# One kernel's output gradient: loaded in four parts, multiplied by the gate row once in SBUF, and w2's gradient copied out by ScalarE

## The chip, the cores and the metric

The kernel runs on one core of one Trainium2 chip. The time is device time of one execution in microseconds (us). The kernel before was run six times: 428.01, 429.35, 428.42, 432.36, 431.66 and 432.61, median 430.51. Less is better.

The engines are named as the profile names them: PE (TensorE, matrix products), DVE (VectorE), ACT (ScalarE), POOL (GpSimd) and SP (SyncE). SP computes nothing; here it issues most of the DMA transfers. Each engine works through its own instructions in a fixed order, and an instruction that waits holds up all that is behind it on that engine.

## The reference

The forward pass is a transformer-like block over x of 2048 rows of 512, conditioned by a vector c: six rows of 512 (sa, ca, ga, sb, cb, gb) come out of c and w_mod. The kernel computes the block's output and the gradients of nine inputs (x, the two halves of the spectral weight, w1, b1, w2, b2, c and w_mod).

```python
    h = _layernorm(x, axis=-1) * (1 + ca) + sa
    x = x + ga * _A_ref(h, A_w_r, A_w_i)      # irfft2(rfft2(h) * W)
    h = _layernorm(x, axis=-1) * (1 + cb) + sb
    x = x + gb * _B_ref(h, B_w1, B_b1, B_w2, B_b2)   # relu(h w1 + b1)^2 w2 + b2
```

With g the gradient of the output, two gradients matter here. That of w2 is the transposed hidden activation (1792 x 2048) times (g * gb), which is 1792 x 512. That of b2 is the sum of (g * gb) over the rows. The row gb is the same for all 2048 rows, so it can be applied to g before the product or to the result after it.

## The kernel before, in words

Everything is bf16 in SBUF and fp32 in PSUM. The 2048 rows lie 16 to a partition: t = 0 to 15 names a slice of 128 rows. The transforms are matrix products with tables of sines. The hidden width 1792 is cut in 14 chunks of 128 (fc), the spectrum in 8 groups (gi).

The kernel goes through a forward spectral stage, then the dense stage in four blocks of 512 rows, forward and backward, and from about 280 us on through the backward spectral part. All that the change touches lies in this last part, which has three stages:

- **Spectral stage** (spec_f23, with ew_b at L1164 and after_b at L1172). For each of eight groups PE makes G, DVE multiplies it with the loaded Z and Xb, writing Z in place and gW into a tile with three buffers, and SP stores gW in four pieces (L1170). after_b then loads what comes later and gives PE units of w1's gradient to fill in (grad_w1, L1122, 16 matmuls of 448 columns each). It also runs GMod.emit four times (gms), which makes a piece of w_mod's gradient from tiles wmc and gwm in the pool gmp.
- **G stage** (spec_g1, L336). For each group PE makes two PSUM tiles psG (four buffers); DVE casts one into the big tile CS (L351), ACT the other (L353). Four small casts of psF by DVE and ACT (L365, L367) finish CS.
- **Row stage** (row_pair, L1267, eight times for t = 0, 2, ... 14: eight pairs). PE makes psT and psY from CS; ACT copies them (Tsb at L377, gs at L1276); DVE unfolds gs into gh (L266 to L270), makes gn (L1278) and q (L1281, which reads the loaded rows n), ACT scales gn (L1280), DVE makes two sums (jk, L1285), gn again (L1289), gs (L1290) and the result gx (L1292, which reads the loaded rows gxl). SP stores gx (L1293) and loads n and gxl for two pairs later (load_rows3, L1219). PE sums gh and q over the rows into acc (L1262), two pairs behind. Between pairs, fill gives PE units of w2's gradient.

A unit of w2's gradient is grad_w2 (L1200): 16 matmuls of one fc, with the transposed load hn (L1067, a DMA that transposes) against g_sb, the output gradient g for all 16 slices, 16 KB in each partition. DVE then reads the PSUM result, multiplies it with the row gb (modb at GB_B) and writes gw (L1206), which SP stores (L1207). b2's gradient is made from g_sb by grad_b2 (L1210) and add_quadrants (L1093), with the row gb applied at its end (L1107).

Memory decides when loads can start. Pools are stacks; a tile placed where an older tile was waits for that tile's last reader or writer. g_sb is placed where gmp was.

The order on each engine is not written out by hand. The framework takes the instructions in program order with priorities and lays them out on the engines by its own estimates of durations; tc.issue_after(x) keeps an instruction from being laid out ahead of x. DMA completion on SP is counted by eight semaphores in rotation, so that an issue also waits until the transfer eight places earlier on its queue has landed.

Of the kernel before, what the change touches and what calls it, by code (L numbers as in the profile page):

```python
# [18 lines left out]
D = 512  # L19
# [315 lines left out]

def spec_g1(tc, K, Z, CS):  # L336
    nc = tc.nc
    with tc.tile_pool(name="psG", bufs=4, space=PSUM) as psG_pool, tc.tile_pool(name="psF", bufs=1, space=PSUM) as psF_pool:
        psF = psF_pool.tile([P, 4, P], FP32, name="psF")
        for gi in range(8):  # L340
            for hh in range(2):
                n = 2 * gi + hh
                ps = psG_pool.tile([P, 2, 2 * P], FP32, name="psG")
                for ch in range(2):
                    for ri in range(2):
                        nc.tensor.matmul(ps[:, ch, :], lhsT=Z[gi][:, hh, ri, ch:256:2],  # L346
                                         rhs=K["LG"][:, n, ri:ri + 2, :].rearrange("p y m -> p (y m)"), start=(ri == 0), stop=(ri == 1))
                dst = CS[:, :, :, n, :].rearrange("p t c b -> p c t b")
                src = ps.rearrange("p h (y t b) -> p (h y) t b", y=2, b=8)
                if hh == 0:  # L350
                    nc.vector.tensor_copy(out=dst, in_=src)  # L351
                else:
                    nc.scalar.copy(out=dst, in_=src)  # L353

            if gi % 2 == 1:
                for ri in range(2):
                    for n in range(2 * gi - 2, 2 * gi + 2):
                        q = 32 * (n % 4)
                        nc.tensor.matmul(psF[q:q + 1, n // 4, :], lhsT=Z[n // 2][:, n % 2, ri, 256:257], rhs=K["LG"][:, n, ri + 1, :],
                                         start=(ri == 0), stop=(ri == 1), tile_position=(0, q))  # L360
        for i in range(4):
            dst = CS[0:1, :, 1, i:16:4, :].rearrange("p t m b -> p m t b")
# [81 lines left out]
class GMod:  # L444
# [12 lines left out]

    def emit(self, jc, q, row, pool, ppool):

# [7 lines left out]
        for dc in range(0, 4, 2):  # L467
            wmc = self.tiles[jc][dc // 2]
            gwm = pool.tile([P, 2, D], BF16, name="gwm", bufs=2)
            for i in range(2):  # L470
# [10 lines left out]
def kernel(  # L481
# [586 lines left out]

    lf2 = tc.alloc_tile_pool(name="lf2", bufs=1, side="right")
    gmp = tc.alloc_tile_pool(name="gmp", bufs=1, side="right")  # L1070
    K["LF"] += [lf2.tile([P, 2, 3, P], BF16, name=f"LFb{gi}") for gi in range(4, 8)]
# [20 lines left out]

    def add_quadrants(ps, pool, out, scale=None):  # L1093
        w = ps.shape[-1]
# [5 lines left out]
        def add():  # L1100
# [4 lines left out]
            nc.scalar.copy(out=row, in_=ps[0:1, 0:w])  # L1105
            if scale is not None:
                nc.vector.tensor_tensor(row, row, scale, op=ALU.mult)  # L1107
            nc.sync.dma_start(out, row)
# [5 lines left out]
    def run_later(n=1):  # L1114
        if later:
            later[0][0] -= n
            if later[0][0] <= 0:
                later.pop(0)[1]()

    w1o = {}  # L1120
# [28 lines left out]
    with tc.tile_pool(name="f23b", bufs=2) as fr, tc.tile_pool(name="ewb", bufs=2) as ew:  # L1149
# [22 lines left out]
        def after_b(gi):  # L1172
            if gi + 4 < 8:
                load(gi + 4)
            if gi == 3:
                with tc.issue_after(K["gW"]):
                    nc.sync.dma_start(K["LG"], LG_dram)
            fill_w1(2 if 0 < gi < 6 else 1)
            if gi == 4:
                with tc.issue_after(K["gW"]):  # L1180
                    load_hn()
                    load_hn()
            if gi == 5:
                gmp.release()
                endp["g"] = tc.alloc_tile_pool(name="gsp", bufs=1, side="right")
                endp["g_sb"] = endp["g"].tile([P, NT, D], BF16, name="g_sb")
                with tc.issue_after(K["gW"]):
                    K["g_load"] = nc.sync.dma_start(endp["g_sb"], g_view).ins
            if gi in (0, 1, 3, 4):
                gms.pop(0)[1]()  # L1190
                if len(gms) > 1:
                    gm.load(gms[1][0], gmp)

        spec_f23(tc, K, UT, AEs, None, lambda gi: gwa.tile([P, 2, 2, FP], BF16, name="G", bufs=2), ew_b, after_b)
    g_sb = endp["g_sb"]
    fin = tc.alloc_tile_pool(name="fin", bufs=2, side="right")
    gwp = tc.alloc_tile_pool(name="gwp", bufs=1, side="right")
    endp["gw"] = gwp

    def grad_w2(fc):  # L1200
# [4 lines left out]
        with tc.high_priority():  # L1205
            nc.vector.tensor_tensor(gw, ps, modb[:, GB_B, :], op=ALU.mult)  # L1206
        nc.sync.dma_start(out6_view[:, fc, :], gw)  # L1207
        load_hn()

    def grad_b2():  # L1210
        ps = psX.tile([P, D], FP32, name="mm")
        for t in range(NT):
            q = 32 * (t % 4)
            nc.tensor.matmul(ps[q:q + 32, :], lhsT=K["ones_q"], rhs=g_sb[:, t, :], start=(t < 4), stop=(t >= 12), tile_position=(0, q))
        add_quadrants(ps, gwp, out_7[None, :], modb[0:1, GB_B, :])

    rows3 = {}

    def load_rows3(t):  # L1219
        if t < NT:  # L1220
            rows3[t] = (fin.tile([P, 2, D], BF16, name="n1"), fin.tile([P, 2, D], BF16, name="gxl"))
            nc.sync.dma_start(rows3[t][0], n1_dram[:, t:t + 2, :])
            nc.sync.dma_start(rows3[t][1], gx1_dram[:, t:t + 2, :])

    with tc.issue_after(K["g_load"]):
        load_rows3(0)
        load_rows3(2)
    for _ in range(2):
        load_hn()

    CS = utcs.tile([P, NT, 4, 16, 8], BF16, name="utcs")
    spec_g1(tc, K, Z, CS)
    sp.release()
# [21 lines left out]
    with tc.tile_pool(name="psE", bufs=2, space=PSUM) as psE, tc.tile_pool(name="psS1", bufs=1, space=PSUM) as psS1:  # L1255
# [41 lines left out]
        for t in range(0, NT, 2):  # L1297
# [4 lines left out]
            if t == 10:  # L1302
                grad_b2()
        fill(1)
        late.flush()
# [5 lines left out]
        for j in range(2):  # L1311
            gm.load(j, endp["gm"])
            gm.emit(j, 32 * j, acc1_sb[32 * j:32 * j + 1, :], endp["gm"], psX)
            fill(1)
# [13 lines left out]
    fp.release()  # L1328
    gwp.release()
    fin.release()  # L1330
    endp["g"].release()
    lf2.release()
# [39 lines left out]
```

## Time and profile before

The profiled execution took 428.01 us; its span, from the first to the last instruction, is 426.2 us. It is the fastest of the six runs.

| | whole span |
|---|---|
| PE busy | 397.4 us, 93% |
| DVE busy | 354.6 us, 83% |
| ACT busy | 256.6 us, 60% |
| POOL busy | 54.9 us, 13% |
| mean DMA rate | 237 GB/s |

The places in the last part: the last unit of w1's gradient ends near 357, the first unit of w2's gradient begins at 357.5, the last matmul of the last unit ends at 421.05.

How to read it: a busy share is an average over stages with different limits. For a stage one looks at each engine's busy time in a stretch of it, and at what its waits were for. In the order of time a row has its start, its length, engine, line, operation, out<-in, and in brackets the idle time before it with what ended it. A DMA appears where it is issued, on SP or POOL; when its data land is another number.

### The profile page before, as it was taken

To read this page: it belongs to the slowest core of one execution; us is meant where nothing else is said; L and a number is where in the kernel's file an instruction comes from. 1 tells how busy PE (TensorE), PEld (TensorE's weight loads), DVE (VectorE), ACT (ScalarE), POOL (GpSimd) and SP (SyncE) were. 2 spreads that over 40 slices of the span, in tenths; PEclk is the share of its full clock that TensorE was granted. 3 is DMA by queue.
4 is the path that set the end of the run, shared out by engine and by line. 5 is a ranking of instruction groups with operands and counts; after the bars stand their busy time and mean duration, and the time that the engine had idled before them with its cause. 6 is when DMAs were issued, how large, how long until landed. Compare 5 with 4: busy or idle time off the path is not lost.

```text
span 426.2 us, 7138 instructions
## 1 busy us (share of the span) xinstructions
PE 397.4 (93%) x2375; PEld 195.9 (46%) x2375; DVE 354.6 (83%) x862; ACT 256.6 (60%) x487; POOL 54.9 (13%) x135
## 2 busy tenths in 40 slices
PE   2789989999899999999999999999999999998895
PEld 0345446654434443444444444445655665443332
DVE  6799858968995588978897998956998848999994
ACT  5578699768883179238824776454755465636331
POOL 8347940000000000000000000002121000000011
PEclk9999999999999999999999999999999999999999
DMA  8998899969397459867985998997999989999993
GB/s 237 242 262 270 246 206 316 319 224 238 105 354 249 136 117 291 244 152 158 313 218 172 133 288 295 295 236 240 302 258 329 213 231 220 206 270 267 257 265 115
DMA packets 144227, 101.11 MB, mean 237 GB/s; under 512 B 98969, under 2 KB 127518, under 8 KB 143806
## 3 DMA queue, kind: packets, MB, share of 16 engines
q1 hardware_dynamic: 141034, 93.03, 83.6%
q0 software_dynamic: 2592, 7.09, 5.3%
q10 hardware_dynamic: 564, 0.53, 0.5%
q8 instruction: 19, 0.31, 0.3%
q14 instruction: 18, 0.15, 0.1%
HBM read 35.44 MB, written 41.60 MB: 181 GB/s over the span
## 4 chain that ended last, share of the span: by engine, by line
PE 50%; DVE 21%; ACT 15%; DMA 8%; issue 4%; POOL 1%; ACTq 0%; DVEq 0%; SPq 0%
PE og L906 12%; PE mm L877 10%; PE mm L1126 7%; PE mm L712 5%; PE mm L1203 4%; DMA out_dram<-gW 3%; DMA xs_dram<-Xs 2%; ACT gab L717 2%; PE psG L346 2%; ACT AE L329 1%; DVE jk L1285 1%; ACT Xs L313 1%; PE acc L774 1%; PE psC L311 1%; DVE l_st L817 1%
## 5 line engine op out<-in xcount | busy, mean ns | idle before, releaser
L712 PE MATMUL mm<-gT,w2T 128*128 128x512 bf16 x224 | 57.9, 383 | 2.9 <-ACT gab L717 2.9
L877 PE MATMUL mm<-h2T,w 128*128 128x512 bf16 x224 | 53.4, 378 | 1.4 <-ACT r L879 1.2
L906 PE MATMUL og<-w1T,gab 128*128 128x512 bf16 x224 | 50.9, 379 | 0.8 <-DVE o L971 0.8
L1203 PE MATMUL mm<-g_sb,hn 128*128 128x512 bf16 x224 | 50.4, 379 | 0.4 <-DVE gw L1206 0.4
L1126 PE MATMUL mm<-gab,h_sb 128*128 128x448 bf16 x256 | 50.7, 352 | 0.0
L906 PE MATMUL og<-w,h 128*128 128x512 bf16 x224 | 50.1, 379 | 0.0
L879 ACT ACTIVATE r<-mm,b1col 128x512 bf16<-128x512 f32 x56 | 37.1, 686 | 6.1 <-PE mm L877 3.3
L877 PEld LDWEIGHTS <-w 128*128 128x128 bf16 x224 | 21.1, 97 | 30.0 <-issue 8.3
L1126 PEld LDWEIGHTS <-h_sb 128*128 128x128 bf16 x256 | 24.6, 98 | 21.8 <-issue 0.6
L906 PEld LDWEIGHTS <-h 128*128 128x128 bf16 x224 | 21.8, 98 | 26.1 <-issue 1.0
L1203 PEld LDWEIGHTS <-hn 128*128 128x128 bf16 x224 | 21.2, 98 | 27.2 <-issue 3.6
L906 PEld LDWEIGHTS <-gab 128*128 128x128 bf16 x224 | 21.6, 98 | 25.9 <-issue 1.4
L712 PEld LDWEIGHTS <-w2T 128*128 128x128 bf16 x224 | 21.3, 99 | 22.5 <-issue 6.3
L919 ACT CAST G<-og 128x512 bf16<-128x512 f32 x16 | 9.2, 581 | 28.1 <-PE og L906 28.1
L295 POOL MEMSET AE<- 128x2 bf16 x4 | 0.3, 102 | 194.3 <-PE mm L877 194.3
L1280 ACT ACTIVATE gs<-gn,inv 128x512 bf16<-128x512 bf16 x16 | 11.4, 716 | 21.8 <-DVE gn L1278 21.8
L477 POOL DMA_DIRECT2D out_dram<-gwm x12 | 8.8, 732 | 114.4 <-DVE gx L1292 54.6
L881 DVE TENSOR_TENSOR h<-r 128x1024 bf16<-128x1024 bf16 x28 | 19.2, 687 | 4.8 <-ACT r L879 4.8
L717 ACT CAST gab<-mm 128x512 bf16<-128x512 f32 x36 | 21.4, 602 | 1.9 <-PE mm L712 1.8
L475 DVE SCALAR_TENSOR_TENSOR gm_junk<-wmc,onef,gmbc 128x512 bf16<-128x512 bf16 x24 | 18.0, 748 | 3.2 <-DMA wmc<-in_w_mod_dram 1.6
L715 DVE CAST gab<-mm 128x512 bf16<-128x512 f32 x20 | 13.8, 688 | 7.7 <-PE mm L712 7.4
L1130 ACT CAST gw<-mm 128x448 bf16<-128x448 f32 x16 | 8.6, 540 | 18.4 <-PE mm L1126 18.4
(290 smaller groups left out, 812.2 us busy)
## 6 DMA issues: line engine op xcount, KB each, us to landing
h_dram<-h SPq DMA_DIRECT2D x28, 256.0 KB, 3.2
gh_dram<-gab SPq DMA_DIRECT2D x28, 256.0 KB, 4.3
w<-in_B_w_dram SPq DMA_DIRECT2D x2, 1792.0 KB
wmc<-in_w_mod_dram SPq DMA_DIRECT2D x12, 256.0 KB, 5.5
out_dram<-gwm POOLq DMA_DIRECT2D x12, 256.0 KB, 6.2
wz_dram<-Z SPq DMA_DIRECT2D x8, 258.0 KB, 4.2
xs_dram<-Xs SPq DMA_DIRECT2D x8, 258.0 KB, 4.3
Z<-wz_dram SPq DMA_DIRECT2D x8, 258.0 KB, 5.3
```

Of the source, the lines that this page charges most:

```text
L475: nc.vector.scalar_tensor_tensor(out=junk, in0=wmc[:, i, :], scalar=K["onef"], in1=gmbc, op0=ALU.mult, op1=ALU.mult, accum_out=self.gsc[:, ...
L712: nc.tensor.matmul(ps, lhsT=w2T[:, dc, fc * P:(fc + 1) * P], rhs=gT[b][:, :, dc, :], start=(dc == 0), stop=(dc == 3))
L715: nc.vector.tensor_copy(out=gaT[b][:, fc, :], in_=ps)
L717: nc.scalar.copy(out=gaT[b][:, fc, :], in_=ps)
L877: nc.tensor.matmul(ps, lhsT=w1[:, dc, (fc + i) * P:(fc + i + 1) * P], rhs=h2T[b][:, :, dc, :], start=(dc == 0), stop=(dc == 3))
L879: nc.scalar.activation(r[:, i, :], ps, AF.Relu, bias=b1col[:, fc + i:fc + i + 1])
L881: nc.vector.tensor_tensor(h2, r, r, op=ALU.mult)
L906: nc.tensor.matmul(ps, lhsT=lhs(fc), rhs=rhs[:, fc, :], start=(fc == 0), stop=(fc == NFC - 1))
L919: nc.scalar.copy(out=st["G"][:, j % 2, :], in_=P_.pop(j))
L1126: nc.tensor.matmul(ps[:, 0:W4], lhsT=h2_sb[:, t, dc * P:(dc + 1) * P], rhs=ghn[t // 4][:, t % 4, fs], start=(t == 0), stop=(t == NT - 1))
L1203: nc.tensor.matmul(ps, lhsT=hns[fc][:, t, :], rhs=g_sb[:, t, :], start=(t == 0), stop=(t == NT - 1))
L1280: nc.scalar.activation(gs[:, i, :], gn[:, i, :], AF.Copy, scale=inv1[:, t + i:t + i + 1], accum_out=rr[:, i, 0:1])
```

## The change

1. g_sb is loaded in four DMAs of 512 KB instead of one of 2 MB, in after_b of group 4 instead of group 5 (so gmp is released at group 4, and the GMod piece of that group is emitted before), and ahead of the first two hn loads, which stood there before.
2. In the G stage DVE multiplies each quarter of g_sb in place with the row gb, one after the cast of each of groups 4 to 7 (scale_g, through the new argument after of spec_g1).
3. Since g_sb then holds g * gb, grad_w2 copies PSUM to gw with ACT, without a product, and add_quadrants loses its product.
4. The rows of the first two pairs (n and gxl, four DMAs of 256 KB) are loaded in after_b of group 3 instead of after the spectral stage. Their pool fin is therefore opened before gmp.
5. The wmc tiles for the last two GMod pieces are loaded at t = 10 and not right before each piece; their gwm tile has four buffers instead of two.

```diff
--- before.py
+++ after.py
@@ -333,7 +333,7 @@
         f3(7)
 
 
-def spec_g1(tc, K, Z, CS):
+def spec_g1(tc, K, Z, CS, after=None):
     nc = tc.nc
     with tc.tile_pool(name="psG", bufs=4, space=PSUM) as psG_pool, tc.tile_pool(name="psF", bufs=1, space=PSUM) as psF_pool:
         psF = psF_pool.tile([P, 4, P], FP32, name="psF")
@@ -348,7 +348,7 @@
                 dst = CS[:, :, :, n, :].rearrange("p t c b -> p c t b")
                 src = ps.rearrange("p h (y t b) -> p (h y) t b", y=2, b=8)
                 if hh == 0:
-                    nc.vector.tensor_copy(out=dst, in_=src)
+                    K["cast"] = nc.vector.tensor_copy(out=dst, in_=src).ins
                 else:
                     nc.scalar.copy(out=dst, in_=src)
 
@@ -358,6 +358,8 @@
                         q = 32 * (n % 4)
                         nc.tensor.matmul(psF[q:q + 1, n // 4, :], lhsT=Z[n // 2][:, n % 2, ri, 256:257], rhs=K["LG"][:, n, ri + 1, :],
                                          start=(ri == 0), stop=(ri == 1), tile_position=(0, q))
+            if after:
+                after(gi)
         for i in range(4):
             dst = CS[0:1, :, 1, i:16:4, :].rearrange("p t m b -> p m t b")
             src = psF[32 * i:32 * i + 1, :, :].rearrange("p m (t b) -> p m t b", b=8)
@@ -455,7 +457,7 @@
         for dc in range(0, 4, 2):
             self.tc.nc.sync.dma_start(self.tiles[jc][dc // 2], self.wm_view[:, dc:dc + 2, cs])
 
-    def emit(self, jc, q, row, pool, ppool):
+    def emit(self, jc, q, row, pool, ppool, nbuf=2):
 
         nc, K = self.tc.nc, self.K
         cs = slice(jc * D, (jc + 1) * D)
@@ -466,7 +468,7 @@
         junk = pool.tile([P, D], BF16, name="gm_junk", bufs=1)
         for dc in range(0, 4, 2):
             wmc = self.tiles[jc][dc // 2]
-            gwm = pool.tile([P, 2, D], BF16, name="gwm", bufs=2)
+            gwm = pool.tile([P, 2, D], BF16, name="gwm", bufs=nbuf)
             for i in range(2):
                 if i == 0:
                     nc.scalar.activation(gwm[:, i, :], gmbc, AF.Copy, scale=self.scf[:, dc + i:dc + i + 1])
@@ -1067,6 +1069,7 @@
             nc.sync.dma_start(hns[fc], h_dram[fc, :, :], transpose=True)
 
     lf2 = tc.alloc_tile_pool(name="lf2", bufs=1, side="right")
+    fin = tc.alloc_tile_pool(name="fin", bufs=2, side="right")
     gmp = tc.alloc_tile_pool(name="gmp", bufs=1, side="right")
     K["LF"] += [lf2.tile([P, 2, 3, P], BF16, name=f"LFb{gi}") for gi in range(4, 8)]
     W4 = 448
@@ -1090,7 +1093,7 @@
         nc.scalar.copy(out=b4, in_=ps[:, 0:W4])
         nc.gpsimd.dma_start(out_5.rearrange("(q f) -> q f", q=NFB), b4[0:P:32, :])
 
-    def add_quadrants(ps, pool, out, scale=None):
+    def add_quadrants(ps, pool, out):
         w = ps.shape[-1]
         b4 = pool.tile([P, w], BF16, name="b4", bufs=1)
         b4l = pool.tile([P, w], BF16, name="b4l", bufs=1)
@@ -1103,8 +1106,6 @@
                 nc.tensor.matmul(ps[0:1, 0:w], lhsT=K["ones_col"], rhs=x, start=(i == 0), stop=(i == 1))
             row = pool.tile([1, w], BF16, name="b4r", bufs=2)
             nc.scalar.copy(out=row, in_=ps[0:1, 0:w])
-            if scale is not None:
-                nc.vector.tensor_tensor(row, row, scale, op=ALU.mult)
             nc.sync.dma_start(out, row)
 
         later.append([4, add])
@@ -1116,6 +1117,14 @@
             later[0][0] -= n
             if later[0][0] <= 0:
                 later.pop(0)[1]()
+
+    rows3 = {}
+
+    def load_rows3(t):
+        if t < NT:
+            rows3[t] = (fin.tile([P, 2, D], BF16, name="n1"), fin.tile([P, 2, D], BF16, name="gxl"))
+            nc.sync.dma_start(rows3[t][0], n1_dram[:, t:t + 2, :])
+            nc.sync.dma_start(rows3[t][1], gx1_dram[:, t:t + 2, :])
 
     w1o = {}
 
@@ -1175,25 +1184,26 @@
             if gi == 3:
                 with tc.issue_after(K["gW"]):
                     nc.sync.dma_start(K["LG"], LG_dram)
+                    load_rows3(0)
+                    load_rows3(2)
             fill_w1(2 if 0 < gi < 6 else 1)
+            if gi in (0, 1, 3, 4):
+                gms.pop(0)[1]()
+                if len(gms) > 1:
+                    gm.load(gms[1][0], gmp)
             if gi == 4:
-                with tc.issue_after(K["gW"]):
-                    load_hn()
-                    load_hn()
-            if gi == 5:
                 gmp.release()
                 endp["g"] = tc.alloc_tile_pool(name="gsp", bufs=1, side="right")
                 endp["g_sb"] = endp["g"].tile([P, NT, D], BF16, name="g_sb")
                 with tc.issue_after(K["gW"]):
-                    K["g_load"] = nc.sync.dma_start(endp["g_sb"], g_view).ins
-            if gi in (0, 1, 3, 4):
-                gms.pop(0)[1]()
-                if len(gms) > 1:
-                    gm.load(gms[1][0], gmp)
+                    for t in range(0, NT, 4):
+                        K["g_load"] = nc.sync.dma_start(endp["g_sb"][:, t:t + 4, :], g_view[:, t:t + 4, :]).ins
+                with tc.issue_after(K["g_load"]):
+                    load_hn()
+                    load_hn()
 
         spec_f23(tc, K, UT, AEs, None, lambda gi: gwa.tile([P, 2, 2, FP], BF16, name="G", bufs=2), ew_b, after_b)
     g_sb = endp["g_sb"]
-    fin = tc.alloc_tile_pool(name="fin", bufs=2, side="right")
     gwp = tc.alloc_tile_pool(name="gwp", bufs=1, side="right")
     endp["gw"] = gwp
 
@@ -1203,7 +1213,7 @@
             nc.tensor.matmul(ps, lhsT=hns[fc][:, t, :], rhs=g_sb[:, t, :], start=(t == 0), stop=(t == NT - 1))
         gw = gwp.tile([P, D], BF16, name="gw", bufs=3)
         with tc.high_priority():
-            nc.vector.tensor_tensor(gw, ps, modb[:, GB_B, :], op=ALU.mult)
+            nc.scalar.copy(out=gw, in_=ps)
         nc.sync.dma_start(out6_view[:, fc, :], gw)
         load_hn()
 
@@ -1212,24 +1222,20 @@
         for t in range(NT):
             q = 32 * (t % 4)
             nc.tensor.matmul(ps[q:q + 32, :], lhsT=K["ones_q"], rhs=g_sb[:, t, :], start=(t < 4), stop=(t >= 12), tile_position=(0, q))
-        add_quadrants(ps, gwp, out_7[None, :], modb[0:1, GB_B, :])
-
-    rows3 = {}
-
-    def load_rows3(t):
-        if t < NT:
-            rows3[t] = (fin.tile([P, 2, D], BF16, name="n1"), fin.tile([P, 2, D], BF16, name="gxl"))
-            nc.sync.dma_start(rows3[t][0], n1_dram[:, t:t + 2, :])
-            nc.sync.dma_start(rows3[t][1], gx1_dram[:, t:t + 2, :])
-
-    with tc.issue_after(K["g_load"]):
-        load_rows3(0)
-        load_rows3(2)
+        add_quadrants(ps, gwp, out_7[None, :])
+
     for _ in range(2):
         load_hn()
 
     CS = utcs.tile([P, NT, 4, 16, 8], BF16, name="utcs")
-    spec_g1(tc, K, Z, CS)
+
+    def scale_g(gi):
+        if gi >= 4:
+            gs = g_sb[:, 4 * gi - 16:4 * gi - 12, :]
+            with tc.issue_after(K["cast"]):
+                nc.vector.tensor_tensor(gs, gs, modb[:, GB_B, None, :].broadcast_to([P, 4, D]), op=ALU.mult)
+
+    spec_g1(tc, K, Z, CS, scale_g)
     sp.release()
     lg2.release()
     fp = tc.alloc_tile_pool(name="fin2", bufs=2, side="right")
@@ -1301,6 +1307,8 @@
             fill(1 if t % 4 == 0 and t < 12 else 0)
             if t == 10:
                 grad_b2()
+                gm.load(0, endp["gm"])
+                gm.load(1, endp["gm"])
         fill(1)
         late.flush()
         acc1_odd = fp.tile([64, D], FP32, name="acc1_odd", bufs=1)
@@ -1309,8 +1317,7 @@
         nc.vector.tensor_tensor(acc1_sb, acc1[0:64, :], acc1_odd, op=ALU.add)
         fill(1)
         for j in range(2):
-            gm.load(j, endp["gm"])
-            gm.emit(j, 32 * j, acc1_sb[32 * j:32 * j + 1, :], endp["gm"], psX)
+            gm.emit(j, 32 * j, acc1_sb[32 * j:32 * j + 1, :], endp["gm"], psX, 4)
             fill(1)
         while units2:
             fill(1)
@@ -1327,8 +1334,8 @@
     psX.release()
     fp.release()
     gwp.release()
+    endp["g"].release()
     fin.release()
-    endp["g"].release()
     lf2.release()
     hnp.release()
     h2p.release()
```

## The prediction

> **What bounds the kernel now.** I read the engine totals, then busy time in 12 us stretches of the last part, then the waits there, and last the SP queue and VectorE in order of time.
>
> The windows first (columns: stretch, length, busy us and count on PE, weight loads, VectorE, ScalarE, GpSimd, clock, DMA share, GB/s):
>
> ```profile
> 346.00:358.00 12.00, 11.98 (x79) 6.58 (x78) 6.08 (x14) 7.99 (x18) 0.86 (x2) 1.00 0.94 201
> 358.00:370.00 12.00, 12.00 (x67) 5.32 (x65) 11.49 (x27) 5.08 (x12) 0.23 (x1) 1.00 1.13 212
> 370.00:382.00 12.00, 12.00 (x74) 5.75 (x71) 11.38 (x30) 6.66 (x16) 0.00 (x0) 1.00 1.00 242
> 382.00:394.00 12.00, 10.98 (x78) 4.88 (x77) 11.59 (x26) 6.74 (x16) 0.00 (x0) 1.00 1.08 275
> 394.00:406.00 12.00, 9.93 (x48) 3.56 (x48) 12.00 (x30) 5.03 (x13) 0.00 (x0) 1.00 1.06 260
> ```
>
> From 358 to 406 VectorE is busy 46.5 of 48 us, and PE loses its only 3.1 us of this part. VectorE's order sets the row stage, but the gain open is small: those 3.1 us, 0.5 elsewhere after 337, and the 5.1 us tail. The DMA rings are occupied throughout.
>
> The waits of three engines, from 282 to the end (engine, line, releaser: total us, times, longest):
>
> ```profile
> DVE q L1281 <- DMA n<-n_dram: 1.5, 2, 1.3
> PE acc L1262 <- DVE gh L270: 1.2, 1, 1.2
> ACT gs L1276 <- DVE gx L1292: 3.8, 1, 3.8
> ```
>
> VectorE already waits for row loads (n), and PE for VectorE's gh of the last row pair. SP issues those loads, in order (start, length):
>
> ```profile
> 336.09 2.51 SPq L1170 DMA_DIRECT2D out_dram<-gW  x4
> 338.84 0.40 SPq L1188 DMA_DIRECT2D g_sb<-in_grad_out_dram  x1
> 339.33 9.24 SPq L1170 DMA_DIRECT2D out_dram<-gW  x8
> ...
> 355.06 6.00 SPq L1067 DMA_TRANSPOSE hn<-h_dram  x2
> 361.16 0.54 SPq L1222 DMA_DIRECT2D n<-n_dram  x1
> 361.74 3.33 SPq L1067 DMA_TRANSPOSE hn<-h_dram  x1
> ...
> 366.21 6.76 SPq L1067 DMA_TRANSPOSE hn<-h_dram  x2
> ```
>
> A transposing load holds SP about 3 us, a plain one 0.3 to 0.5. The n of pair 2 (rows 4, 5) goes out at 361.16, between transposes. VectorE uses it here, and PE's wait ends with the second line:
>
> ```profile
> 369.56 0.69 DVE L1281 TENSOR_TENSOR q<-gh,n 128x1024 bf16<-128x1024 bf16 x1
> ...
> 402.56 0.42 DVE L270 TENSOR_TENSOR gh<-unf_u 128x512 bf16<-128x512 bf16 x1
> ```
>
> [...] 14 hn transposes, 1.93 to 5.68 us, median 3.33. [...] gW stores issued before g_sb landed in 5.5 us, those behind it in 10.4 to 10.8. [...] L1206 from PSUM takes 685 ns for 512 elements, L1278 from SBUF 689 ns for 1024.
>
> **The change, part by part.**
>
> 1. VectorE loses the 14 gw copies. Starts follow each other by 0.60 us; 7 lie between 369.56 and gh at 402.56, so 4.2 us off the stretch that PE waits on. b4r's 0.41 goes too, beside other work.
>
> 2. VectorE gains four multiplications of 128x2048. Spacing is 0.34 us at 512 elements and 0.60 at 1024, so 1.13 at 2048 [...]: 4.5 us. The built program puts them after the casts (L351) of groups 4 to 7. Cast 4 ends at 342.9, so cast 5 ends at 344.7, when PE wants its buffer (there are four); psF's casts end at 352 instead of 348.6. PE is covered: 31 grad_w1 matmuls, not 14, now precede the first psT (17 more x 0.19 = 3.2 us), costing it 0.2, or 3.4 without that cover. VectorE's row stage starts at 354.9, not 351.6.
>
> 3. ScalarE gains 14 copies of about 0.586 (as gmbc, L465); busy 5 to 8 of 12 us, it has room. Each waits for a PE unit with Tsb, gs and L1280 queued behind it, and VectorE waits for those: I take 1.0 us over pairs 0 to 2. Bounds 0 and 2.5; no gain, since nothing is shortened there.
>
> 4. g_sb's four loads move from behind group 5's gW to behind group 4's and ahead of hn0 and hn1. The first waits for the last gwm stores (324.75 + 7.8 = 332.6). In ring order I place the landings at 339 to 343.5, an estimate from 2 MB in some 6 us; the multiplications want them from 342.9 to 348.2. Cost 0; up to 3 us if late, since casts stand behind.
>
> 5. The first four row loads (1 MB) move from 349.8-353.4 to behind LGb, at 322 to 327. That removes VectorE's 1.3 us wait for n at pair 0. They go past group 4's gW, whose stores free the buffer that VectorE writes for group 7 at 338.6: landing about 334 before, some 337.4 with 1 MB at 0.3 MB/us ahead. Margin 1.2, cost 0; up to 2 us if lost, since all psG casts are behind.
>
> 6. What is displaced decides. SP's order in the built program is now: group 4's gW, g_sb x4, hn0, hn1, gW of groups 5 to 7, then **hn2 to hn6 in a row, and only then n of pair 2**. hn2 waits for the landing of group 7's gW (355.06 before). The rows' 1 MB formerly landed after that, about 355 to 357.6, and now lies ahead of it in saturated rings: hn2 starts at 357.6 (bounds 352, if the rings had slack, and 360). Five transposes at 3.33: n goes out at 374.2. With 3.2 us to its use, as for pair 3 (issued 373.69, used 376.85), it is there at **377.4**.
>  VectorE wants it earlier: from 354.9 it has pair 0 (6.1), pair 1 without gs and gx (4.9), pair 2 to gn (2.0) and the 1.0 of part 3, so 368.8. A new wait of 8.6 us.
>
> 7. From that q to the last pair's gh took 33.4 us (369.56 to 402.98). Less 4.2 (part 1), plus 1.2 as gs and gx of pair 1 now follow q: 30.4, so gh at 407.8. From gh to the last matmul took 18.1 (to 421.05), the same work after: 425.9, that is +4.9. Behind n of pair 2 SP has one transpose, three stores or so, a gxl and two wmc loads ahead of n of pair 3, out at 380.5 and landing about 385 (4.6, the median of such loads), wanted at 384.5: +0.5.
>
> 8. The last two wmc tiles load at row 10 and gwm gets four buffers: it ends ScalarE's 0.3 us wait for a gwm store, beside PE's last units: 0. They add to SP ahead of pair 3's n, counted above. The last gw copy is 0.1 shorter but its store follows gcr: 0. The order of pool releases: 0.
>
> Sum: **+5.4 us**. The profiled execution took 428.01 (span 426.2 and 1.8 around it), so 433.4. It is the fastest of six; the median of the runs is 430.51, and on it I put the difference: **435.9**.
>
> **Rivals.**
>
> A, relief reaches the end. If n of pair 2 is there by 368.8, gh comes at 399.3 and PE, arriving there at 398.7, ends by 418.2: -2.9, 427.6. For it: single transposes took 2.25 and 2.37, so five may take 12 us, and hn2 may start by 352. Against: pairs in a row took 6.00 to 8.54. The point of decision: n there at 402.98 - 30.4 = 372.6; earlier is not slower. Chance 0.17.
>
> B, half absorbed: hn2 at 355 as before, 3.0 us a transpose: n at 373.2, +0.6, 431.1 (429.5 to 432.5). Chance 0.21.
>
> C, the G stage is hit as well: group 4's gW or g_sb lands 2 to 3 us late, VectorE's casts wait, PE's four psG buffers fill. +2.6 on the forecast: 438.5 (437.5 to 441). For it: my margin of 1.2. Against: hn0 and hn1 no longer lie ahead of g_sb. Chance 0.17.
>
> The forecast itself, 432.5 to 437.5, has 0.45.
>
> **How the numbers follow.** One per cent, 4.3 us, is about what a measurement of this kernel can tell from no change. Slower than 434.8: all of C and most of the forecast, 0.58. Faster than 426.2: only if A also shortens the tail, 0.03. The rest, 0.39. The range leaves out the best half of A and the worst of C: 429.0 to 440.5. The forecast's own range stands above.
>
> **What would show it.** Right: q (L1281's successor) of pair 2 idle 5 us or more on a load of n; five transposes in a row on SP, n after them; PE idle near 375 to 382 before psY of pair 4 and at the last acc; no gw group on VectorE, one of 14 near 0.59 on ScalarE; four of about 1.2 us in the G stage. Wrong: n landed before VectorE asks, transposes in a row taking 2.4 us or less, or PE idle already in the G stage.

## The result, and the profile after

The kernel after takes 433.36 us (median of 36 runs, 431.65 to 437.42), the kernel before 431.01 (73 runs, 427.72 to 434.30). The ratio is 1.0064, 95% interval 1.0049 to 1.0079, so some 2.8 us slower: a small loss, but one clear of the noise, and about half of the 5.4 us forecast. The profiled execution took 435.55 us, span 433.7.

The same 12 us stretches as before, of after (stretch, length, busy us and count on PE, weight loads, VectorE, ScalarE, GpSimd, clock, DMA share, GB/s):

```profile
346.00:358.00 12.00, 11.86 (x84) 6.65 (x83) 7.61 (x12) 6.34 (x12) 0.54 (x1) 1.00 0.68 133
358.00:370.00 12.00, 12.00 (x72) 5.80 (x70) 11.04 (x29) 8.61 (x19) 0.54 (x1) 1.00 0.76 160
370.00:382.00 12.00, 6.09 (x37) 2.73 (x35) 5.08 (x15) 3.81 (x9) 0.00 (x0) 0.91 1.12 221
382.00:394.00 12.00, 12.00 (x68) 5.23 (x70) 9.89 (x24) 6.06 (x14) 0.00 (x0) 0.81 0.91 275
394.00:406.00 12.00, 11.24 (x74) 4.72 (x67) 10.95 (x28) 7.70 (x19) 0.00 (x0) 1.00 1.03 235
```

From 370 to 382 PE stands for half of the time, VectorE and ScalarE for more than half. The next stretch has a PE that is busy throughout, at a clock of 0.81; before, the clock was 1.00 everywhere here.

The waits after, from 282 on (total us, times, longest), and below them SP and VectorE in order of time:

```profile
DVE q L1287 <- DMA n<-n_dram: 8.5, 2, 6.9
...
PE psY L387 <- ACT Tsb L379: 6.6, 2, 5.9
...
PE acc L1268 <- DVE gh L270: 1.4, 1, 1.4
```

```profile
347.48 8.57 SPq L1179 DMA_DIRECT2D out_dram<-gW  x12
360.83 13.19 SPq L1069 DMA_TRANSPOSE hn<-h_dram  x5
374.06 0.58 SPq L1126 DMA_DIRECT2D n<-n_dram  x1
```

```profile
377.50 0.69 DVE L1287 TENSOR_TENSOR q<-gh,n 128x1024 bf16<-128x1024 bf16 x1 [6.85 <-DMA n<-n_dram]
...
386.62 0.69 DVE L1287 TENSOR_TENSOR q<-gh,n 128x1024 bf16<-128x1024 bf16 x1 [1.63 <-DMA n<-n_dram]
```

The five transposes in a row, n behind them, and VectorE's wait for it are there as forecast; ScalarE's Tsb and PE's psY stand behind VectorE. The second q line is that of pair 3, which waits as well.

Both kernels were profiled a second time on another chip (spans 424.0 and 428.4). The table cuts the four profiles at the same events, each at its start; the difference is after less before, first pair and second. The forecast to the last gh has the 0.5 us wait of pair 3 in it.

| us | before | before, 2nd | after | after, 2nd | difference, pairs | forecast |
|---|---|---|---|---|---|---|
| start to first psG | 337.08 | 335.87 | 337.94 | 335.67 | +0.9, -0.2 | 0 |
| to q of pair 2 | 32.48 | 31.50 | 39.56 | 36.06 | +7.1, +4.6 | +7.8 |
| to the last gh | 33.00 | 32.98 | 32.80 | 33.16 | -0.2, +0.2 | -2.5 |
| to the last matmul | 18.40 | 18.40 | 19.93 | 20.05 | +1.5, +1.7 | 0 |
| to the end | 5.24 | 5.25 | 3.47 | 3.46 | -1.8, -1.8 | 0 |
| span | 426.2 | 424.0 | 433.7 | 428.4 | +7.5, +4.4 | +5.4 |

All three terms behind the wait for n came out otherwise than forecast, in both directions. From PE's side, from the first psG to the last matmul, it was busy 80.3 us before in both profiles, 82.8 and 83.6 after with the same work, and idle 3.6 and 2.6 before, 9.5 and 5.7 after. The busy time grew because PE's clock fell to 0.50 after it had stood, for 6.8 us in each of the two profiles of after. That is not a cost on top of the table: at its last sum of gh PE still waits 1.4 us for VectorE in the first profile of after, and comes 0.3 us late in the second, and VectorE waits for none of PE's work on the way there. So the slow clock took little more than time that PE would have stood.

The profiles' differences exceed that of the medians: both profiled executions of before were under its median, by 3.0 and 2.7 us, and the first of after was 2.2 us above its own. What an ordinary execution of before loses is not to be seen in them, and stays open.

### The profile page after: what moved, and what is told of

Same layout as the page of the kernel before. It is cut to its first block, busy times and chain, and to the rows that moved or that the text cites. A ratio compares the mean times of both kernels' runs of the same rounds, so it can differ in the third digit from the quotient of the medians.

```text
span 433.7 us, 7151 instructions
## 1 busy us (share of the span) xinstructions
PE 398.9 (92%) x2375; PEld 196.0 (45%) x2375; DVE 350.6 (81%) x851; ACT 264.1 (61%) x501; POOL 54.6 (13%) x135
## 4 chain that ended last, share of the span: by engine, by line
PE 30%; DVE 24%; ACT 17%; DMA 15%; SPq 5%; issue 5%; POOL 2%; ACTq 0%; DVEq 0%
PE og L908 9%; PE mm L879 5%; PE mm L714 4%; PE mm L1213 4%; DMA out_dram<-gW 4%; SPq L1069 3%; DMA LGb<-LG_dram 2%; DMA xs_dram<-Xs 2%; ACT gab L719 2%; ACT AE L329 2%; DMA n<-n_dram 2%; DMA wmc<-in_w_mod_dram 1%; ACT Xs L313 1%; ACT n2rows L942 1%; DMA y<-gx_dram 1%
## 5 line engine op out<-in xcount | busy, mean ns | idle before, releaser
L1213 PE MATMUL mm<-g_sb,hn 128*128 128x512 bf16 x224 | 51.7, 386 | 0.2 <-ACT gw L1216 0.2
L714 PEld LDWEIGHTS <-w2T 128*128 128x128 bf16 x224 | 21.2, 98 | 22.9 <-issue 6.8
L379 ACT ACTIVATE Tsb<-psT 128x512 bf16<-128x512 f32 x32 | 18.5, 607 | 3.0 <-PE psT L377 2.0
L887 DVE TENSOR_TENSOR gab<-r,gab 128x1024 bf16<-128x1024 bf16 x28 | 19.2, 685 | 0.0
```

What stands on the lines that cost most here:

```text
L379: nc.scalar.activation(Tsb, ps, AF.Copy, scale=EF_S)
L714: nc.tensor.matmul(ps, lhsT=w2T[:, dc, fc * P:(fc + 1) * P], rhs=gT[b][:, :, dc, :], start=(dc == 0), stop=(dc == 3))
L887: K["gh"] = nc.vector.tensor_tensor(gh, r, gh, op=ALU.mult).ins
L1213: nc.tensor.matmul(ps, lhsT=hns[fc][:, t, :], rhs=g_sb[:, t, :], start=(t == 0), stop=(t == NT - 1))
```

## The experiments

They ran in three groups on three chips (before's medians 430.64, 428.23 and 428.45), so ratios to the kernel before are compared; a ratio 0.01 higher is some 4.3 us, and the expectations in us are on the scale of some 430.6. n_first, n_second, no_mult, gw_dve, rows_pool, rows3b and fed are edits of the kernel after; b_relief, b_rows and b_rows3 of the kernel before.

| run | ratio to before | 95% interval |
|---|---|---|
| after, on the third chip | 1.0051 | 1.0030 to 1.0072 |
| n_first | 0.9973 | 0.9947 to 0.9999 |
| n_second | 1.0040 | 1.0022 to 1.0058 |
| no_mult | 1.0000 | 0.9978 to 1.0022 |
| gw_dve | 1.0089 | 1.0051 to 1.0127 |
| b_relief | 1.0013 | 0.9990 to 1.0036 |
| b_rows | 0.9983 | 0.9963 to 1.0003 |
| rows_pool | 1.0042 | 1.0017 to 1.0066 |
| rows3b | 0.9943 | 0.9923 to 0.9963 |
| fed | 1.0114 | 1.0082 to 1.0146 |
| b_rows3 | 0.9967 | 0.9952 to 0.9983 |

**Where n stands in SP's queue (n_first, n_second).**

```diff
-            nc.sync.dma_start(hns[fc], h_dram[fc, :, :], transpose=True)
+            with tc.issue_after(K["n"][4] if fc >= 4 else K["g_load"]):
+                nc.sync.dma_start(hns[fc], h_dram[fc, :, :], transpose=True)
...
-                gm.load(0, endp["gm"])
-                gm.load(1, endp["gm"])
+                with tc.issue_after(K["n"][4]):
+                    gm.load(0, endp["gm"])
+                    gm.load(1, endp["gm"])
```

K["n"][4] is the load of n for t = 4 and 5, that is pair 2. In n_second the bound is 5 instead of 4.

> Edit: the transposing loads hn4 to hn6 are issued behind n of pair 2, instead of ahead of it; the last wmc loads are held behind it as well, so that they don't take the free place. All else as in the kernel after. Theory 1 (the queue on SP): the whole loss is n's wait of 6.85 us. n goes out after hn2 and hn3, at about 360.8 + 2 x 2.64 = 366.1 in the clock of the profile after, is there at 369.4, and VectorE wants it at 370.6: no wait. The last gh comes some 6 us earlier, and the whole takes 427 to 428.5 us. Theory 2 (work): VectorE's four multiplications and the late start of its row stage set the time; the load only fills what was idle anyway: no change, 433 us within 1. Theory 3 (half and half): a new wait (hn4 late for PE, or n of pair 3 late) takes the place of it: 430 to 431.5.

> Edit: as the kernel with n of pair 2 behind two transposes, but with one transpose more (hn4) ahead of n. Theory 1: n goes out 2.64 us later, at 368.8, lands at 372.0 and leaves a wait of about 1.4 us: 1.4 us above the kernel with two ahead, 428.5 to 430. Theory 2: no change against the kernel after, 433. Theory 3: the same as with two ahead, since another wait then decides.

n_first is 0.9% faster than after, 3.9 us. That is less than the 5 to 6 us of theory 1, and the reason is in SP's and VectorE's order of time:

```profile
359.60 4.23 SPq L1070 DMA_TRANSPOSE hn<-h_dram  x2
363.87 0.58 SPq L1127 DMA_DIRECT2D n<-n_dram  x1
...
374.99 0.51 SPq L1127 DMA_DIRECT2D n<-n_dram  x1
```

```profile
368.88 0.68 DVE L1288 TENSOR_TENSOR q<-gh,n 128x1024 bf16<-128x1024 bf16 x1
...
379.03 0.69 DVE L1288 TENSOR_TENSOR q<-gh,n 128x1024 bf16<-128x1024 bf16 x1 [2.67 <-PE mm L1214]
```

q of pair 2 waits for nothing. q of pair 3 now waits 2.67 us: the named PE had long been done, and it is n of pair 3, issued at 374.99 behind hn4 to hn6. So the wait has moved one pair on: theory 3's mechanism, at a time just under its 430 to 431.5. In n_second, with one transpose more ahead of n, q of pair 2 waits 1.98 us, near the 1.4 expected. But hn7 has slipped ahead of n of pair 3 as well (six transposes ahead of it in all, not five), and q of pair 3 waits 4.22. The time, 432.3, is nearer to theory 2's 433 than to theory 1's, though not for theory 2's reason: the waits for n are back.

**What the multiplications cost (no_mult).**

```diff
-    spec_g1(tc, K, Z, CS, scale_g)
+    spec_g1(tc, K, Z, CS)
```

> Edit: the four multiplications with the gate row in the G stage are left out, and nothing takes their place, so the factor is missing from w2's and b2's gradient. In the built program this also moves n of pair 2 from behind hn6 to behind hn3 on SP. Theory 1: the gain is that of the place of n (427 to 428.5) and at most 1.5 us more, since hn2 starts no earlier: 426 to 428. Theory 2: VectorE's row stage starts 3.4 to 4.5 us earlier and the end follows by as much: 429 to 430. What tells them apart further is the difference to the kernel that keeps the multiplications and has n at the same place: theory 1 expects under 1.5 us, theory 2 3.4 to 4.5 us.

Without 4.9 us of VectorE's work it is no faster than n_first, which keeps it: 1.0000 against 0.9973. That speaks against theory 2, but the pair is not clean: in no_mult the built order gives VectorE 31.4 us of work from q of pair 2 to the last gh, in n_first 29.5. With the multiplications the built program has n's load behind hn6, without them behind hn3. That the framework's estimate of a later VectorE moved it is the likely reason, argued only. A cleaner pair follows below (rows3b and b_rows3).

**What the relief is worth (b_relief, gw_dve).** The first pair of lines is b_relief, an edit of the kernel before; the second is gw_dve, of the kernel after.

```diff
-            nc.vector.tensor_tensor(gw, ps, modb[:, GB_B, :], op=ALU.mult)
+            nc.scalar.copy(out=gw, in_=ps)
...
-            nc.scalar.copy(out=gw, in_=ps)
+            nc.vector.tensor_copy(out=gw, in_=ps)
```

> Edit: the kernel before, with its 14 gw copies done by ScalarE as plain copies; the gate factor is missing from w2's gradient. Loads and their order on SP stay as before up to n of pair 2. This is the relief alone. Theory 1 (the relief is worth its VectorE time, 7 copies of 0.60 us up to the last gh, as the prediction had it): 4.2 us less, 426.5. Theory 2 (the loads of n keep VectorE's pace, so that it only waits longer for them: n of pair 3 landed just when it was wanted, and n of pair 4 0.2 us late): of the relief only the copies behind pair 4's q count, four of 0.60 us at most, and ScalarE's waits take some back: 428.5 to 430.5. Theory 3: the copies on ScalarE hold up Tsb and gs so much that nothing is left: 430.6 or more.

> Edit: the 14 copies of w2's gradient go back to VectorE, as plain copies; ScalarE is free of them. SP's order up to n of pair 2 is unchanged. Theory 1: VectorE waits for n until the same moment, and then has some 6 to 7 copies of 0.60 us more up to the last gh: +3.6 to +4.2 us against the kernel after, 437 to 437.5. Theory 2: as the row stage is bound by VectorE throughout, also +4 to +5: 437.5 to 438.5. Theory 3 (PE and the DMA rings set the row stage, VectorE only follows): within 1 us of the kernel after.

At the end nothing is left of the relief: 1.0013, and putting the copies back on VectorE costs 0.25% with intervals that overlap, not the 0.8 to 1.2% of theories 1 and 2. Here is VectorE from q of pair 2 to the last gh, first of before, then of b_relief: the window (columns as above), and what jk waited for in it.

```profile
369.56:402.56 33.00, 30.61 (x186) 13.40 (x185) 31.97 (x76) 16.80 (x39) 0.00 (x0) 1.00 1.03 255
...
DVE jk L1285 <- ACT gs L1280: 0.3, 1, 0.3
```

```profile
370.19:405.01 34.82, 30.39 (x186) 13.30 (x185) 31.43 (x75) 20.18 (x46) 0.00 (x0) 1.00 1.01 253
...
DVE jk L1285 <- ACT gs L1280: 2.1, 6, 0.4
```

Seven copies are gone from it, some 4.2 us, but VectorE is busy only 0.5 us less: the built order has moved other work in (two gn, a gs and a gx more than before). And jk waits 2.1 us for ScalarE, not 0.3. So b_relief is not the relief alone. gw_dve shows the layout from the other side: there the stretch is 2.6 us longer than in after, but 57 matmuls of w2's gradient are left for PE behind the last gh instead of 78.

One pair shows such a wait, again first of before, then of b_relief:

```profile
376.85 0.69 DVE L1281 TENSOR_TENSOR q<-gh,n 128x1024 bf16<-128x1024 bf16 x1
377.45 0.68 DVE L1206 TENSOR_TENSOR gw<-mm,modb 128x512 bf16<-128x512 f32 x1
378.06 0.74 DVE L1285 SCALAR_TENSOR_TENSOR jk<-gs,onef,n 128x512 bf16<-128x512 bf16 x1
```

```profile
377.45 0.69 DVE L1281 TENSOR_TENSOR q<-gh,n 128x1024 bf16<-128x1024 bf16 x1
378.48 0.75 DVE L1285 SCALAR_TENSOR_TENSOR jk<-gs,onef,n 128x512 bf16<-128x512 bf16 x1 [0.34 <-ACT gs L1280]
```

jk reads what ScalarE makes of gn, and follows q by 1.21 us with the copy between them and by 1.03 without. Of the 0.60 us that this copy took, 0.18 is gained; most of the rest has become a wait for ScalarE.

**The early rows alone (b_rows).** The kernel before, with the loads at group 3.

```diff
                     nc.sync.dma_start(K["LG"], LG_dram)
+                    load_rows3(0)
+                    load_rows3(2)
...
-    with tc.issue_after(K["g_load"]):
-        load_rows3(0)
-        load_rows3(2)
```

> Edit: the kernel before, with the row loads of pairs 0 and 1 issued at group 3 behind LGb, as in the kernel after; all else as before. SP still has n of pair 2 behind hn2 and hn3. Theory 1: VectorE's wait for n at pair 0 goes (1.3 us), and that for group 7's gW buffer may come (0.7 us in the kernel after): 429.5 to 431.5. Theory 2 (the 1 MB moved ahead is what delays the transposes and all behind them, as the prediction's step 6 took it for hn2): hn2 starts 2 to 5 us later than before and n of pair 2 with it: 432 to 434.

Theory 1: 0.9983, and the wait for n at pair 0 is gone (q of pair 3 waits 0.9 us for its own). hn2 goes out 18.2 us after the first psG (353.97 against 335.79), as before (18.0). The early rows bring no stall; with n behind hn3 the kernel stays as it was or gains a little. In after hn2 goes out 22.9 us after the first psG in one profile and 18.2 in the other; b_rows gives no sign that the early rows delay it. Something else has changed there: hn0 and hn1 (8.3 us on SP) now stand behind g_sb and ahead of the last twelve gW stores, the last of which goes out at 355.45 (before at 347.97), and hn2 waits 4.5 us for these to land. This was not tested by itself.

**The loads off SP (rows_pool).**

```diff
-            nc.sync.dma_start(rows3[t][0], n1_dram[:, t:t + 2, :])
-            nc.sync.dma_start(rows3[t][1], gx1_dram[:, t:t + 2, :])
+            q = nc.sync if t < 4 else nc.gpsimd
+            q.dma_start(rows3[t][0], n1_dram[:, t:t + 2, :])
+            q.dma_start(rows3[t][1], gx1_dram[:, t:t + 2, :])
```

> Edit: the kernel after, with the row loads n and gxl of pairs 2 to 7 issued by GpSimd, which has little to do by then, instead of SP. They are no longer behind any transpose; each goes out when its buffer is free. Theory 1 (the queue on SP costs the time): n of pair 2 goes out at about 363, when gn of pair 0 is done, and no q waits more than 1 us: 426.5 to 428.5. Theory 2 (the rings are full, and a load lands as late from another queue): waits for n of 2 us and more stay, 431 to 433.5. Theory 3 (issuing from GpSimd is itself slow): n lands, but gxl and the n of later pairs come late: 429 to 431.

No q waits for n any more, and it is still 1.0042. SP and VectorE in order of time:

```profile
356.01 16.35 SPq L1069 DMA_TRANSPOSE hn<-h_dram  x5
372.41 0.58 SPq L1218 DMA_DIRECT2D out_dram<-gw  x1
373.04 0.43 SPq L1300 DMA_DIRECT2D out_dram<-gx  x1
```

```profile
378.17 0.69 DVE L1299 TENSOR_TENSOR gx<-gs,gxl 128x1024 bf16<-128x1024 bf16 x1 [3.87 <-DMA out_dram<-gx]
```

The store of pair 0's gx stands behind the same five transposes, and gx has two buffers, so pair 2's gx waits 3.87 us for it. The queue takes its toll at another DMA; none of the three theories had named that one, though the time lies where theory 2 put it.

**The queue mended (rows3b, b_rows3).**

```diff
-            rows3[t] = (fin.tile([P, 2, D], BF16, name="n1"), fin.tile([P, 2, D], BF16, name="gxl"))
-            nc.sync.dma_start(rows3[t][0], n1_dram[:, t:t + 2, :])
...
+    def load_n(t):
+        if t < NT:
+            pool = endp["fp"] if t % 6 == 4 else fin
+            rows3[t] = pool.tile([P, 2, D], BF16, name="n1", bufs=1 if t % 6 == 4 else 2)
+            K["n"] = K[f"n{t}"] = nc.sync.dma_start(rows3[t], n1_dram[:, t:t + 2, :]).ins
...
+    with tc.issue_after(K["gW"]):
+        load_n(4)
...
+            load_n(t + 6)
...
-            nc.sync.dma_start(hns[fc], h_dram[fc, :, :], transpose=True)
+            with tc.issue_after(K["n6"] if fc >= 5 else K["n4"] if fc >= 2 else K["g_load"]):
+                nc.sync.dma_start(hns[fc], h_dram[fc, :, :], transpose=True)
```

The load of n for six rows on stands in row_pair behind the last use of n.

> Edit: the kernel after, with a third buffer for n, so that n of pair 2 goes out ahead of hn2 and n of pair t+3 as soon as pair t is done; hn5 and later ones are held behind n of pair 3, and the last wmc loads behind n of pair 4. All on SP. Theory 1: no q of pairs 2 and 3 waits, the last gh comes 3 us earlier than with only hn4 to hn6 held back (402.7 in that profile), and the whole takes 426 to 427.5. Theory 2 (with the loads in time something else sets the pace: ScalarE's order, or PE's order of units): within 1 us of that kernel, 429 to 430.5.

> Edit: the kernel before, with the early row loads, the third buffer for n and the transposes held behind n of pairs 2 and 3, as in the kernel that did best; VectorE still makes gw with the factor, g_sb is loaded in one. This tells what the change itself is worth once no n waits behind a transpose. Theory 1 (the relief of VectorE counts once the queue is mended): 1 to 2 us slower than that kernel, ratio to before 0.997 to 0.999. Theory 2 (the relief is worth nothing, the gain is the queue's): the same as that kernel, ratio 0.993 to 0.996.

rows3b is the fastest of all: 0.9943, on its chip 425.65 us against 428.23. No q of it waits for a load. Its waits from 322 on that touch PE, and SP:

```profile
PE acc L1277 <- DVE gh L270: 1.4, 1, 1.4
...
PE psY L387 <- ACT Tsb L379: 0.8, 1, 0.8
```

```profile
355.02 6.97 SPq L1070 DMA_TRANSPOSE hn<-h_dram  x3
362.04 0.58 SPq L1133 DMA_DIRECT2D n<-n_dram  x1
362.67 2.86 SPq L1070 DMA_TRANSPOSE hn<-h_dram  x1
```

From the first psG to the last matmul it takes 83.3 us, PE idle for 2.9 of them. b_rows3, the kernel before with the same queue, takes 82.9 there, PE idle for 2.6, but 5.25 instead of 3.46 us from the last matmul to the end. VectorE from q of pair 2 to the last gh, of rows3b and of b_rows3:

```profile
367.91:399.41 31.50, 29.68 (x183) 12.97 (x182) 29.52 (x73) 20.23 (x46) 0.00 (x0) 1.00 1.03 256
```

```profile
369.27:402.25 32.98, 31.60 (x190) 13.75 (x189) 31.85 (x76) 16.80 (x39) 0.00 (x0) 1.00 1.06 257
```

No q waits for a load in either, so this pair shows what VectorE's part of the change is worth. Counted from the first psG, rows3b with its multiplications has q of pair 0 3.3 us later, but q of pair 2 only 0.35. VectorE is then busy 2.3 us less up to the last gh, which follows q of pair 2 1.5 us sooner. But the kernel doesn't end earlier for it: in PE's order 78 matmuls of w2's gradient stand behind the last gh instead of 72, and PE waits for that gh 1.4 us instead of 1.2. PE has some 80.3 us of work from the first psG to the last matmul in both.

So once the queue is mended the row stage gains nothing, and what is left of the change is its tail: 0.24% or 1 us, with intervals that overlap. Both runs came out between their theories 1 and 2. b_rows3 itself is 0.33% faster than before, but its profile agrees with the second one of before within 0.1 us in every row of the table behind the first psG; where an ordinary execution of before loses that is not seen.

**PE's clock (fed, and all profiles).** The edit is on after; K["w2"] is the last matmul of w2's gradient so far.

```diff
             fill(1)
+            if t == 8:
+                px = psX.tile([P, D], FP32, name="mm")
+                with tc.issue_after(K["w2"]):
+                    for _ in range(24):
+                        nc.tensor.matmul(px, lhsT=K["ident"], rhs=g_sb[:, 0, :], start=True, stop=True)
             row_pair(t, Ts)
```

> Edit: the kernel after, with 24 matmuls 128x512 whose result nobody reads, on PE directly ahead of the psY of pair 4 that stood idle for 5.91 us. They take 24 x 0.22 = 5.3 us of that idle time. In the profile after, PE's clock fell to 0.50 from about 379 and came back by 387. Theory 1 (PE's standing still brings the clock down): with PE fed the clock stays at 1.00, and the kernel loses only the wait: of the 7 us at half clock 5 lie on PE's work, so 2.4 us less than after, a ratio to before near 1.000 to 1.003, mean clock above 0.996. Theory 2 (the clock falls for another reason, and the idle time before it is chance): the clock falls as before, mean 0.991, ratio 1.006 to 1.009.

> Edit: none, the kernel after on the chip of these runs, as an anchor for the two others and for a second profile. Both theories of the half clock expect PE's idle time ahead of psY of pair 4 again, with 4 to 7 us at 0.50 behind it; ratio to before 1.005 to 1.008.

> Edit: none, a second profile of the kernel before, since the first is of an execution 2.5 us under the median. Expected of an ordinary one: the same order, with n of pair 2 and pair 3 landing up to 2.5 us later, or the loads of the G stage, and at most one short fall of the clock.

Stretches of 2 us of after around its idle time, and of fed at the same place:

```profile
376.00:378.00 2.00, 0.00 (x0) 0.00 (x0) 0.50 (x1) 0.00 (x0) 0.00 (x0) 1.00 0.97 337
...
380.00:382.00 2.00, 0.19 (x1) 0.10 (x1) 1.93 (x8) 1.82 (x4) 0.00 (x0) 0.50 1.07 247
382.00:384.00 2.00, 2.00 (x13) 0.75 (x12) 2.00 (x6) 1.04 (x3) 0.00 (x0) 0.50 0.90 273
384.00:386.00 2.00, 2.00 (x9) 0.90 (x8) 0.95 (x2) 1.19 (x4) 0.00 (x0) 0.50 0.88 278
```

```profile
376.00:378.00 2.00, 2.00 (x11) 0.94 (x10) 2.00 (x6) 1.49 (x4) 0.00 (x0) 1.00 0.97 269
378.00:380.00 2.00, 2.00 (x13) 0.73 (x11) 1.72 (x4) 0.15 (x1) 0.00 (x0) 1.00 0.92 300
380.00:382.00 2.00, 2.00 (x19) 1.15 (x16) 1.71 (x4) 2.00 (x6) 0.00 (x0) 1.00 1.06 373
406.00:408.00 2.00, 0.00 (x0) 0.00 (x0) 2.00 (x5) 0.00 (x0) 0.00 (x0) 1.00 0.69 170
408.00:410.00 2.00, 1.78 (x5) 0.43 (x4) 1.62 (x4) 1.01 (x3) 0.00 (x0) 0.51 1.20 309
```

The clock falls to 0.50 in the idle time of after. With PE fed it stays at 1.00 there, and falls later, behind 2.75 us in which PE was not fed. That is theory 1 for the clock. Over all runs on this chip the mean clock of the span was 0.997 with PE fed (6 runs), 0.994 in after (21) and 0.998 in before (42), falls behind the last matmul included.

The time went against theory 1: 1.0114. The 5.3 us were cut to PE's 5.91 us of idle time in the first profile; in this execution n kept VectorE only 3.30 us, and no idle time was left ahead of psY. The built order also gave VectorE 32.5 us of work from q of pair 2 to the last gh, not 29.5, and the fall came behind the last gh, where PE alone sets the time. So fed tells of the clock, and not of what a full clock would save; in the two profiles of after PE's lateness at the last gh (none, and 0.3 us) says that it would be little.

The second profile of after again had a gap, of 3.20 us, with a fall behind it. The second profile of before was meant to show an ordinary execution and caught a faster one, in which no q waits.

## Why the prediction was right, and where its sum was not

The time lies in the forecast's range, 432.5 to 437.5, and the wait that it rests on is there. That the sum came so near is in part luck: its errors went both ways.

- **Steps 1 to 3, counts and durations**: right. The four multiplications took 1216 ns each at a spacing of 1.13, the 14 copies 582 ns on ScalarE, and psF's casts moved late without hurting PE. VectorE asked for n of pair 2 32.7 and 31.9 us after the first psG in the two profiles, forecast 31.7.
- **Step 4** (g_sb): right. No multiplication waited for it. The 6 us for 2 MB were the author's estimate; in the first profile of after the second to fourth quarter landed in the order of their issue, at 342.4, 343.7 and 345.0, some 1.3 us apart. One reading that the ring order leans on was short: of the gW stores behind g_sb one took 11.5 us, over the 10.4 to 10.8 given.
- **Step 5** (rows at group 3): the 1.3 us at pair 0 went, though the second profile of before doesn't have that wait either. Its 0.3 MB/us is near the 298 GB/s that before moved from 318 to 334. The margin of 1.2 us for group 7's gW was lost in the first profile (0.7 us of VectorE, 1.1 of PE), but not in the second.
- **Step 6** (the queue): right that five transposes ahead of n make VectorE wait. In the first profile it is right even in place: n out at 374.06 (forecast 374.2), q at 377.50 (377.4). Two errors cancelled there, which is luck: hn2 started at 360.83 instead of 357.6, and five transposes took 13.2 us, not 16.7. In the second profile hn2 went out 18.2 us after the first psG, not 22.9, and five took 14.6. The wait was 6.85 us and 4.15, not 8.6. Its reason for a later hn2, the rows' 1 MB, is not borne out by b_rows.
- **Step 7** was mis-sized. *Up to the last gh* VectorE's work shrank by 2.4 us, near the 3.0 forecast. But jk waited for ScalarE 1.1 us (0.3 and 0.7 before), which the step put at nothing behind pair 2, and n of pair 3 was waited for 1.6 and 2.0 us, not 0.5. Together these took back the relief: -0.2 and +0.2. *The 18.1 us from gh to the last matmul* grew by 1.5 to 1.7, as the built order left 78 matmuls of w2's gradient behind the last gh instead of 72 (6 x 0.22 = 1.3; the rest is not explained). *The clock* was taken as constant; it fell for 6.8 us in both profiles of after, but ahead of the last gh, where it cost next to nothing.
- **Step 8** failed in the other direction: the tail was put at 0 and shrank by 1.8 us. The last instructions of before and of after:

```profile
421.07 0.69 DVE L1206 TENSOR_TENSOR gw<-mm,modb 128x512 bf16<-128x512 f32 x1 [0.38 <-PE mm L1203]
421.68 0.20 DVE L1325 COPY gcr<-mm 4x128 bf16<-4x128 bf16 x1
422.22 0.29 SPq L1326 DMA_DIRECT2D out_dram<-gcr  x1
```

```profile
430.33 0.59 ACT L1216 CAST gw<-mm 128x512 bf16<-128x512 f32 x1 [2.87 <-PE mm L1213]
430.48 0.21 DVE L1332 COPY gcr<-mm 4x128 bf16<-4x128 bf16 x1 [4.44 <-PE mm L1330]
430.72 0.28 SPq L1333 DMA_DIRECT2D out_dram<-gcr  x1
431.10 0.34 SPq L1217 DMA_DIRECT2D out_dram<-gw  x1
```

gcr no longer queues behind gw on VectorE: its store goes out 0.49 us behind the last matmul, not 1.26, and the large store follows instead of preceding it. The span ends 2.6 us after the last store goes out, not 4.0. All nine profiles with ScalarE's copy, b_relief among them, have about 3.5 to 3.75 us from the last matmul to the end, the four of before's form about 5.25, gw_dve 4.2. That the order of the two stores makes the last 1 us is argued only.

Rival A, with n in time, was put at 427.6. n_first is that case for pair 2 and took 429.93: pair 3's wait of 2.67 us took the place of the relief. rows3b, where no q waits, is 2.4 us faster than before, near A's 2.9; but b_rows3 has 1.4 of them without the change.

## What to carry to other kernels

Ask of every load in a stage what is laid out ahead of it on its queue. Here a transposing load held the queue for some 2.6 us, and five of them ahead of one row load undid the change. After an edit on one engine read the queue's built order again: it may have moved.

Work taken off a busy engine counts at the end only as far as another engine's idle time allows. VectorE was busy 97% of the row stage, but PE was idle for only 2.6 to 3.6 us of some 83, and the layout can move its units to either side of the wait. Before multiplying counts by durations, look too at whether the work fills waits of a chain with another engine.

And follow the last output to its landing: most of 1.8 us came there from two copies that no longer share an engine.

## What the runs showed of the hardware

The granted clock fell to 0.50 behind gaps in PE's work: for 3.4 us in nine falls and for 6.8 in one, the first profile of after, where PE stood longest (5.91 us). In the fourteen profiles, from 322 on and ahead of the last matmul (a gap just ahead of it in gw_dve is left out), it fell with all seven gaps of 2.58 to 5.9 us, three of six from 1.6 to 2.2 and none of thirteen from 1.0 to 1.42. A fall began within its gap or up to 1.8 us behind it. What a fall costs depends on where it lies: behind the last gh it went with 1.6 to 1.7 us (fed and b_relief took that much longer there than before, with the same 72 matmuls of w2's gradient). In the six profiles where it fell ahead of the last gh, PE still waited 1.4 to 1.7 us for that gh in four, and was 0.3 us late in two.

A row of five transposing loads took SP 11.8 to 16.4 us in five profiles with the same order (2.4 to 3.3 each). In the two of the same program the longer row (14.6 against 13.2 us) went with the shorter wait for n, as hn2 started 4.7 us earlier.

In before, n of pair 0 goes out at 349.79, when the gW store eight places ahead of it on SP, issued at 339.33, has landed (10.4 us after its issue).
